# Two columns of W1I in one pass, scores read from PSUM, and the last bank stored whole

## The chip, the cores and the metric

The kernel runs on one core of a Trainium2 chip. The metric is the device time of one execution in microseconds (us); lower is better. The engines are named as the profile names them: PE (matmul) with PEld (its weight loads), DVE (vector), ACT (scalar), POOL, and SP, whose queue issues most DMAs. Each engine runs its own instructions strictly in the order in which the program holds them and waits for others by semaphores.

## The reference

```python
def reference(q, k, v, tau, moe..., moe2...):
    # q, k, v: 1 x 6016 x 256; w_in: 256 x 2048, w_out: 2048 x 256 (twice)
    qn = q / (norm(q, axis=1) + 1e-06);  kn = k / (norm(k, axis=1) + 1e-06)
    s = kn.transpose(0, 2, 1) @ qn / tau          # 256 x 256
    a = exp(s - s.max(-1));  a /= a.sum(-1) + 1e-09
    x = v @ a                                      # 6016 x 256
    h = x @ w1_in;  x = (h * sigmoid(1.702 * h)) @ w1_out
    h = x @ w2_in;  return (max(h, 0) + alpha * min(h, 0)) @ w2_out
```

All in float32. The kernel never makes `v @ a`: it multiplies `a` into the first layer's weight (`W1I = a @ w1_in`, called `WI` in the code) and feeds v's tokens to that.

## The kernel before

**Precision.** Every float32 operand is held as a pair hi + lo of fp32r tiles, and a product is three matmuls (`PASSES`): hi by hi, hi by lo, lo by hi. So each operand costs a cast on ACT (hi) and a subtraction on DVE (lo) before PE may use it.

**Head.** From 7 to 48 us PE accumulates the gram matrix k^T q in two PSUM banks, `gram[0]` and `gram[1]` (lines 340 to 349). At its end `nrm` holds the sums of squares, `rr` the reciprocal norms, and two matmuls spread q's reciprocal norms over the partitions into the PSUM bank `bc` (L447). ACT copies `bc` times 1/tau to `rq` (L448). `scores(m)` on DVE multiplies gram m by `rq` and k's factor and takes the maximum (L458); `exponent(m)` is on ACT (L463); `turn(m)` transposes the result on PE (`pt`, L472) and splits it into `eT_hi` (ACT, L477) and `eT_lo` (DVE, L476).

**W1I.** Output j of W1I (a column block of 256 of the 2048) is made by `make_w(j, m, ...)` for the two halves m: six matmuls of 256 columns each, `eT` by the converted weight `wi_pair[j]`, into a bank `pw` (L484). `keep_hi` (ACT, L492) and `keep_lo` (DVE, L496) store it to `WI`. The input weights come as raw 64-bit words, and a `Convert` piece turns them to hi and lo in steps: on ACT `scale` (L130) and `copy` (the cast to hi, L143), on DVE `shift` (L133), `signed` (L137), `power` (L147), `rest` (L150), `less` (L166) and `low` (L169, which writes lo). `ia[j]` is the piece of output j's input weight (outputs 4 and 5, and 6 and 7, share one of twice the width), `ob_[j]` that of the output weight. The `Converter` takes the pieces in one fixed order, ia1, ob0, ia2, ob1, ia3, ob2, ia4, ..., and does a step or two wherever the program calls `beside`; `conv.need(pieces)` emits at that place all steps still missing, up to those pieces.

**First token block.** `direct(j, outs, mid_way)` runs j from 0 to 7 over tokens 0 to 1023. Each has four units i = 0 to 3 (two rows of 128 features by two token chunks); here unit (j, i) names one. A unit is two `product` calls of three matmuls into a bank `ps_h` (L670) and, between them, two groups of three matmuls into `ps_o` for the unit (j-1, i) before (L699): 12 matmuls of 512 columns on PE. Then ACT applies the activation (`g`, L748) and casts `ghi` (L762), `mid_way(i)` is called, `beside` puts in some converter steps, and DVE makes `glo` (L768). `mid_way(1)` calls `emit_w(j + 1)`: the W1I of the next j is made behind unit (j, 1), two units ahead of its first use by unit (j + 1, 0).

**The rest.** All other tokens go through `quartet`, seven products for eight blocks (Strassen's way), for layer 1 and then layer 2. At the end `evacuate` copies the finished banks out; the last bank goes in two halves of 224 columns, each with its copy on ACT (L717) and its DMA on SP's queue (L718).

Of the kernel before, what the change touches and what calls it, by code (L numbers as in the profile page):

```python
# [8 lines left out]
F32 = mybir.dt.float32  # L9
F32R = mybir.dt.float32r  # L10
U32 = mybir.dt.uint32
AF = mybir.ActivationFunctionType
ALU = mybir.AluOpType
AX = mybir.AxisListType

P = 128
N = 6016
C = 256
FF = 2048
NT = FF // P  # L20
NQ = NT // 2
R = N // P
T = 512
# [11 lines left out]
TAIL = 12  # L35
ON_VECTOR = (4, 5, 6, 8)
assert sum(QK_PARTS) == R
PASSES = ((0, 0), (0, 1), (1, 0))
# [5 lines left out]
def f32(ap):  # L44
    return ap.bitcast(F32)
# [6 lines left out]
def flat(ap):  # L52
    return ap.rearrange("p a b -> p (a b)")
# [3 lines left out]
def attention_then_two_ffns(ctx: ExitStack, tc: tile.TileContext, q, k, vT, tau, w1i, w1o, w2i, w2o, alpha, outT):  # L57
# [14 lines left out]
    nc = tc.nc  # L72
# [12 lines left out]
    tau_sb = const.tile([P, 1], F32, name="tau_sb")  # L85
# [17 lines left out]
    class Convert:  # L103
# [64 lines left out]
        def low(self):  # L168
            nc.vector.tensor_tensor(self.lo, self.like(self.top), self.like(self.p), ALU.add)  # L169
            self.made = True  # L170
            if self.done:
                self.done()
# [73 lines left out]
    conv = Converter()  # L246
# [8 lines left out]
    with tc.manual_schedule():  # L255
# [2 lines left out]
        smx = ExitStack()  # L258
        Convert.pool = smx.enter_context(tc.tile_pool(name="cw", bufs=1, side="right"))
        sm = smx.enter_context(tc.tile_pool(name="sm", bufs=1, side="right"))  # L260
        wi_pair = {}

        def wi_tiles():
            return [sm.tile([P, 2, PIECE], F32R, tag=f"wi{h}", name=f"wi_{h}") for h in ("hi", "lo")]

        wi_first = [wi_tiles()]
        ident = sm.tile([P, P], F32, name="ident")
        ones = sm.tile([P, P], F32, name="ones")
        ET = tuple(sm.tile([P, 2, 2, P], F32R, name=f"eT_{h}") for h in ("hi", "lo"))

        def inner(j, n=1):
            def pair():
                if j % 2 == 0:
                    t = wi_first.pop() if wi_first else wi_tiles()
                    for i in range(2):
                        wi_pair[j + i] = tuple(x[:, :, i * C:(i + 1) * C] for x in t)
                    if n == 2:
                        return [flat(x) for x in t]
                return wi_pair[j]
            return Convert(w1i.rearrange("p (a n) -> p a n", a=2)[:, :, j * C:(j + n) * C], pair)  # L280
# [6 lines left out]
        ia, ob_ = {}, {}  # L287
# [8 lines left out]
        G = sm.tile([P, 2, C], F32, name="G")  # L296
# [3 lines left out]
        rs = sm.tile([P, 2], F32, name="rs")  # L300
# [12 lines left out]
        def operand(pool=None):  # L313
            if pool:
                return pool.tile([P, 2, T], F32R, tag="x", name="x")
            i = slot[0] % 11
            slot[0] += 1
            return xin[i > 3].tile([P, 2, T], F32R, tag=f"x{i}", name="x")
# [4 lines left out]
        def high(h, c):  # L323
            blocks[h, c] = operand()
            nc.scalar.copy(blocks[h, c][:, 0], raws[0, c][:, h])
# [5 lines left out]
        with ExitStack() as pre:  # L331
# [8 lines left out]
            gram = [pso.tile([P, T], F32, tag="o", name=f"gram{m}") for m in range(2)]  # L340
# [3 lines left out]
            def emit_gram(these, halves):  # L344
                for t in these:
                    i, r = rows[t]
                    for m in halves:
                        nc.tensor.matmul(gram[m][:, :C], tiles[i][:, 1, r, m * P:(m + 1) * P], tiles[i][:, 0, r, :],  # L348
                                         start=(t == 0), stop=(t == R - 1))
# [71 lines left out]
            rr = sm.tile([P, 4], F32, name="rr")  # L421
            high(0, 0)
            for h in range(2):
                add(norms[:, h], summed[:, h], acc[:, h])
                for j in range(2):
                    nc.tensor.matmul(nrm[:, 2 * h + j:2 * h + j + 1], norms[:, h, j * P:(j + 1) * P], ones[:, 0:1],  # L426
                                     start=True, stop=True)
            conv.steps(2)
            put_off.pop(0)()
            conv.steps(2)  # L430
            conv.load()
# [10 lines left out]
            bc = pso.tile([P, T], F32, tag="o", name="bc")  # L442
            rq = sm.tile([P, C], F32, name="rq")
            conv.steps(1)
            emit_gram(range(R - TAIL, R - TAIL + 4), (1,))
            for j in range(2):
                nc.tensor.matmul(bc[:, j * P:(j + 1) * P], rr[:, j:j + 1].to_broadcast([P, P]), ident, start=True, stop=True)  # L447
            nc.scalar.activation(rq, bc[:, :C], AF.Copy, scale=tau_sb)  # L448
            low(0, 0)
            high(1, 0)  # L450
        psh = ctx.enter_context(tc.tile_pool(name="psh", bufs=4, space=bass.MemoryType.PSUM))
        xin.append(ctx.enter_context(tc.tile_pool(name="xin1", bufs=1)))
        wti = ctx.enter_context(tc.tile_pool(name="wti", bufs=1))
# [1 line left out]
        WI = wti.tile([P, NQ, 2, 7, P], F32R, name="wi")  # L455

        def scores(m):
            nc.vector.tensor_tensor_reduce(G[:, m], gram[m][:, :C], rq, rr[:, 2 + m:3 + m], -3e38, ALU.mult, ALU.max,  # L458
                                           mx[:, m:m + 1])

        def exponent(m):
            nc.scalar.activation(mx[:, m:m + 1], mx[:, m:m + 1], AF.Copy, scale=-1.0)
            nc.scalar.activation(G[:, m], G[:, m], AF.Exp, bias=mx[:, m:m + 1], accum_out=sums[:, m:m + 1])  # L463
# [5 lines left out]
        def turn(m):  # L469
            pt = pso.tile([P, T], F32, tag="o", name="pt")  # L470
            for j in range(2):
                nc.tensor.transpose(pt[:, j * P:(j + 1) * P], G[:, m, j * P:(j + 1) * P], ident)  # L472
            hi, lo = (t[:, m].rearrange("p j c -> p (j c)") for t in ET)

            def rest():
                nc.vector.tensor_tensor(lo, pt[:, :C], f32(hi), ALU.subtract)  # L476
            nc.scalar.copy(hi, pt[:, :C])  # L477
            return rest

        def make_w(j, m, pw, at=0):  # L480
            n = 0
            for a, b in PASSES:
                for i in range(2):
                    nc.tensor.matmul(pw[:, at:at + C], ET[a][:, m, i], wi_pair[j][b][:, i],  # L484
                                     start=(n == 0), stop=(n == 5), skip_group_check=True)
                    n += 1
# [4 lines left out]
        def keep_hi(j, m, pw, at=0):  # L491
            nc.scalar.activation(next(kept(j, m)), pw[:, at:at + C], AF.Copy, scale=rs[:, m:m + 1])  # L492

        def keep_lo(j, m, pw, at=0):
            hi, lo = kept(j, m)
            nc.vector.scalar_tensor_tensor(lo, pw[:, at:at + C], rs[:, m:m + 1], f32(hi), ALU.mult, ALU.subtract)  # L496

        scores(0)
        exponent(0)
        emit_gram(range(R - TAIL + 4, R - 1), (1,))  # L500
        conv.steps(1)
        high(0, 1)
        scalar_work()
# [1 line left out]
        low(1, 0)  # L505
        low(0, 1)
        rest0 = turn(0)
        emit_gram((R - 1,), (1,))
        high(1, 1)
        rest0()  # L510
        assert ia[0].made and ia[1].made
# [105 lines left out]
        def combine_wi(j):  # L617
            return combine(*(WI[:, j, h, :4] for h in range(2)), *(lambda h=h: WI[:, j, h, S1:] for h in range(2)))

        def emit_w(j):  # L620

            conv.need([ia[j]])
            pw = psh.tile([P, T], F32, tag="h", name="pw") if j > 1 else pw_next
            for m in range(2):
                if j > 1 or m:
                    make_w(j, m, pw, m * C)
            for m in range(2):
                if j > 1 or m:
                    keep_hi(j, m, pw, m * C)
                    keep_lo(j, m, pw, m * C)  # L630
# [45 lines left out]
        acc_ps = {}  # L676
# [29 lines left out]
        def evacuate():  # L706

            while ready:
                l, c = ready.pop(0)
                n, t0 = WIDTHS[c], starts[c]  # L710
                for d in range(2):
                    dst = outT[d * P:(d + 1) * P, t0:t0 + n] if l else x1[c][:, d]
                    copies = (nc.scalar.copy, nc.vector.tensor_copy)
                    if l and d and c == len(WIDTHS) - 1:
                        for at in (slice(0, n // 2), slice(n // 2, n)):
                            ob = sp.tile([P, T], F32, tag="s", name="s", bufs=3)
                            nc.scalar.copy(ob[:, :n // 2], acc_ps[c][d][:, at])  # L717
                            nc.sync.dma_start(dst[:, at], ob[:, :n // 2])  # L718
                        continue
                    ob = sp.tile([P, T], F32, tag="ob", name="ob", bufs=4)  # L720
                    copies[d](ob[:, :n], acc_ps[c][d][:, :n])
                    nc.sync.dma_start(dst, ob[:, :n])
# [195 lines left out]
        for j in range(NQ):  # L918
            if j:
                conv.need([ob_[j - 1]])  # L920

            def mid_way(i):
                if j < NQ - 1 and i == 1:
                    if j == 0:
                        conv.need([ob_[0]])
                    emit_w(j + 1)
                if j == 2 and i == 0:
                    nc.sync.dma_start(alpha_sb, alpha)
                if j == 3 and i < 2:
                    load_tokens(0, 2 + i)  # L930
                if j == 5 and i == 0:
                    early, late = prepare(0, 1)
                    bg.extend(early + late)
                    for n in range(AHEAD):
                        combined.append(combine_wi(n))
                        bg.extend(combined[n])

            outs = direct(j, outs, mid_way)
# [4 lines left out]
        sp = ctx.enter_context(tc.tile_pool(name="sp", bufs=3, side="right"))  # L943
# [143 lines left out]
```

## Time and profile before

| | before |
|---|---|
| time, median of 3 runs (lowest to highest) | 1034.88 us (1034.62 to 1034.90) |
| the profiled execution: its own time / its span | 1034.92 us / 1033.2 us |
| PE busy | 1027.2 us (99%) |
| DVE busy / ACT busy | 766.1 us (74%) / 753.5 us (73%) |
| chain that ended last, by engine | PE 99% |
| matmuls on PE | 4664 |

Times in the rows count from the first instruction of the span. Matmuls are pipelined: a row's duration is longer than the distance to the next matmul, so what one costs is read from the distance between starts, or from the chain, whose pieces do not overlap.

### The profile page before, as it was taken

Reading aid. Unit: us, or ns where it says so; the run is one execution under the profiler, and the core shown is the slowest. Engines: PE = TensorE matmul, PEld = TensorE weight load, DVE = VectorE, ACT = ScalarE, POOL = GpSimd, SP = SyncE. Lnnn points to the kernel's source line nnn. Section 1 sums busy time; section 2 is a strip of 40 time slices with the busy share of each in tenths; the row PEclk is TensorE's granted clock in tenths of the full one; section 3 lists DMA queues with packets and bytes.
Section 4 is the critical chain, followed back from the end, with each engine's and each line's share of the span. In section 5 each row is a group of like instructions: output and inputs, shape, how many; then the busy total and the mean of one; then the engine's idle time right before and its main releaser. Section 6 shows DMA issues by size and latency. Waiting matters only on the chain.

```text
span 1033.2 us, 12543 instructions
## 1 busy us (share of the span) xinstructions
PE 1027.2 (99%) x4664; PEld 868.0 (84%) x4664; DVE 766.1 (74%) x1233; ACT 753.5 (73%) x1259; POOL 31.3 (3%) x42
## 2 busy tenths in 40 slices
PE   9999999999999999999999999999999999999998
PEld 8888888888888888888998888888888888888997
DVE  5789977878778787445637777787877787877765
ACT  6776667778777777666767777777777777867776
POOL 4400000000000000000110000000000000000000
PEclk9999999999999999999999999999999999999999
DMA  9635012125224323003543001001001000000101
GB/s 359 242 105 180 1 63 96 41 77 179 77 82 158 99 95 133 0 1 122 204 169 113 1 21 62 1 21 62 0 21 62 1 18 25 35 1 1 42 0 36
DMA packets 30605, 77.62 MB, mean 75 GB/s; under 512 B 3024, under 2 KB 7760, under 8 KB 30288
## 3 DMA queue, kind: packets, MB, share of 16 engines
q1 hardware_dynamic: 28240, 65.29, 18.1%
q0 software_dynamic: 2304, 11.54, 3.3%
q8 instruction: 36, 0.59, 0.2%
q14 instruction: 25, 0.20, 0.1%
HBM read 52.96 MB, written 23.86 MB: 74 GB/s over the span
## 4 chain that ended last, share of the span: by engine, by line
PE 99%; DMA 0%; SPq 0%; issue 0%; ACT 0%; ACTq 0%
PE ps_o L699 50%; PE ps_h L670 44%; PE gram L348 4%; PE pw L484 1%; DMA qk<-in_k 0%; SPq L368 0%; PE nrm L426 0%; PE bc L447 0%; PE pt L472 0%; ACT s L717 0%; ACTq L1083 0%
## 5 line engine op out<-in xcount | busy, mean ns | idle before, releaser
L699 PE MATMUL ps_o<-ghi,wo 128*128 128x512 f32 (+1 forms) x1536 | 562.5, 386 | 0.0
L670 PE MATMUL ps_h<-x,wi 128*128 128x512 f32 (+1 forms) x2040 | 550.7, 386 | 0.0
L670 PEld LDWEIGHTS ps_h<-x,wi 128*128 128x128 f32 x2040 | 382.2, 188 | 71.8 <-DVE wi L496 0.4
L699 PEld LDWEIGHTS ps_o<-ghi,wo 128*128 128x128 f32 x1536 | 288.6, 188 | 53.6
L699 PE MATMUL ps_o<-glo,wo 128*128 128x512 f32 (+1 forms) x768 | 296.5, 386 | 0.0
L737 DVE TENSOR_TENSOR g<-ps_h,s 128x512 f32<-128x512 f32 (+1 forms) x177 | 120.1, 678 | 94.0 <-PE ps_h L670 60.4
L766 DVE SCALAR_TENSOR_TENSOR glo<-g,sign_sb,ghi 128x512 fp32r<-128x512 f32 (+1 forms) x192 | 141.4, 737 | 55.4 <-ACT ghi L760 51.1
L803 ACT COPY s<-ps_h 128x512 f32<-128x512 f32 (+1 forms) x177 | 102.2, 577 | 104.6 <-PE ps_h L670 100.4
L768 DVE TENSOR_TENSOR glo<-g,ghi 128x512 fp32r<-128x512 f32 (+1 forms) x192 | 126.4, 677 | 67.5 <-ACT ghi L762 67.1
L699 PEld LDWEIGHTS ps_o<-glo,wo 128*128 128x128 f32 x768 | 144.3, 188 | 26.9 <-DVE glo L766 0.3
L760 ACT ACTIVATE ghi<-g,sign_sb 128x512 fp32r<-128x512 f32 (+1 forms) x192 | 137.0, 714 | 16.3 <-DVE g L756 10.9
L762 ACT CAST ghi<-g 128x512 fp32r<-128x512 f32 (+1 forms) x192 | 113.2, 611 | 3.6
L748 ACT ACTIVATE g<-ps_h 128x512 f32<-128x512 f32 (+1 forms) x112 | 65.5, 585 | 37.4 <-PE ps_h L670 36.7
L752 ACT ACTIVATE g<-g,sign_sb 128x512 f32<-128x512 f32 (+1 forms) x97 | 69.5, 717 | 29.1 <-DVE g L737 28.6
L756 DVE SCALAR_TENSOR_TENSOR g<-g,slope_sb 128x512 f32<-128x512 f32 (+1 forms) x97 | 71.6, 739 | 16.8 <-ACT g L752 16.6
L756 DVE SCALAR_TENSOR_TENSOR g<-ps_h,slope_sb,g 128x512 f32<-128x512 f32 (+1 forms) x95 | 69.7, 734 | 0.0
L814 ACT COPY ps_h<-ps_h 128x512 f32<-128x512 f32 (+1 forms) x87 | 49.0, 563 | 28.4 <-PE ps_h L670 27.8
L752 ACT ACTIVATE g<-ps_h,sign_sb 128x512 f32<-128x512 f32 (+1 forms) x95 | 64.2, 676 | 2.0 <-PE ps_h L670 0.2
L748 ACT ACTIVATE g<-g 128x512 f32<-128x512 f32 (+1 forms) x80 | 49.8, 623 | 15.5 <-DVE g L737 15.3
L348 PE MATMUL gram<-qk 128*128 128x256 f32 x156 | 34.3, 381 | 1.0 <-DMA qk<-in_k 1.0
L348 PEld LDWEIGHTS gram<-qk 128*128 128x128 f32 x156 | 29.5, 190 | 5.2 <-issue 1.4
L561 DVE TENSOR_TENSOR x<-t,x 128x512 fp32r<-128x512 f32 (+1 forms) x44 | 29.0, 672 | 0.0
(104 smaller groups left out, 504.7 us busy)
## 6 DMA issues: line engine op xcount, KB each, us to landing
wi<-w2i POOLq DMA_DIRECT2D x8, 896.0 KB, 4.9
xraw<-in_vT SPq DMA_DIRECT2D x10, 512.0 KB, 6.1
x<-ob SPq DMA_DIRECT2D x20, 256.0 KB, 2.4
xraw<-x SPq DMA_DIRECT2D x10, 512.0 KB, 3.5
out_T<-ob SPq DMA_DIRECT2D x20, 256.0 KB, 2.1
qk<-in_q SPq DMA_DIRECT2D x9, 512.0 KB, 10.2
qk<-in_k SPq DMA_DIRECT2D x9, 512.0 KB, 10.3
raw<-in_w2i SPq DMA_DIRECT2D x8, 512.0 KB, 4.1
```

What stands on the lines that cost most here:

```text
L348: nc.tensor.matmul(gram[m][:, :C], tiles[i][:, 1, r, m * P:(m + 1) * P], tiles[i][:, 0, r, :], start=(t == 0), stop=(t == R - 1))
L670: nc.tensor.matmul(ps[:, :n], WI[:, wq, a, blk], x[:, b, :n], start=(start and i == 0), stop=(stop and i == 2), skip_group_check=True)
L699: nc.tensor.matmul(acc_ps[c][d][:, :n], WO[:, j, a, f, d * P:(d + 1) * P], (hi, lo)[b][:, :n], start=(start and i == 0), stop=(stop and i ...
L737: nc.vector.tensor_tensor(self.src, ps[:, :self.n], s[:, :self.n], ALU.add)
L748: nc.scalar.activation(self.g, self.src, AF.Gelu_apprx_sigmoid)
L752: nc.scalar.activation(self.g, self.src, AF.Copy, scale=sign_sb[:, self.f])
L756: nc.vector.scalar_tensor_tensor(self.g, self.src, slope_sb[:, self.f], self.g, ALU.mult, ALU.max)
L760: nc.scalar.activation(self.hi, self.g, AF.Copy, scale=sign_sb[:, self.f])
L762: nc.scalar.copy(self.hi, self.g)
L766: nc.vector.scalar_tensor_tensor(self.lo, self.g, sign_sb[:, self.f], f32(self.hi), ALU.mult, ALU.subtract)
L768: nc.vector.tensor_tensor(self.lo, self.g, f32(self.hi), ALU.subtract)
L803: nc.scalar.copy(s[:, :n], ps[:, :n])
```

## The change

Three edits. First, `emit_pair(j)` makes outputs j and j + 1 of W1I at once, with matmuls of 512 columns and one bank for each half m, and with one `hi` and one `lo` instruction for each half. Outputs 2 to 7 go this way: `mid_way(2)` of j = 1, 3 and 5 calls `emit_pair(j + 1)`; output 1 stays with `emit_w`. Second, in the head ACT copies `gram[0]` to `G` early, 1/tau goes into k's factors `rr[:, 2:4]`, `scores(0)` reads q's factors from `bc` itself, and the copy to `rq` comes behind `exponent(0)`; one step of the gram moves behind the first transposes. Third, the last bank is stored by one copy and one DMA.

```diff
@@ inner / head
-                    t = wi_first.pop() if wi_first else wi_tiles()
+                    t = wi_whole[j] = wi_first.pop() if wi_first else wi_tiles()
...
             conv.steps(2)
+            nc.scalar.copy(G[:, 0], gram[0][:, :C])
             put_off.pop(0)()
...
-            nc.scalar.activation(rq, bc[:, :C], AF.Copy, scale=tau_sb)
-            low(0, 0)
-            high(1, 0)
+            nc.vector.tensor_scalar(rr[:, 2:4], rr[:, 2:4], tau_sb, None, ALU.mult)
...
         def scores(m):
-            nc.vector.tensor_tensor_reduce(G[:, m], gram[m][:, :C], rq, rr[:, 2 + m:3 + m], ...
+            nc.vector.tensor_tensor_reduce(G[:, m], *((gram[1][:, :C], rq) if m else (G[:, 0], bc[:, :C])), rr[:, 2 + m:3 + m], ...
...
         scores(0)
         exponent(0)
-        emit_gram(range(R - TAIL + 4, R - 1), (1,))
+        nc.scalar.copy(rq, bc[:, :C])
+        high(1, 0)
+        low(0, 0)
+        emit_gram(range(R - TAIL + 4, R - 2), (1,))
...
         rest0 = turn(0)
-        emit_gram((R - 1,), (1,))
+        emit_gram((R - 2, R - 1), (1,))
@@ W1I
+        def emit_pair(j):
+            conv.need([ia[j], ia[j + 1]])
+            for m in range(2):
+                pw = psh.tile([P, T], F32, tag="h", name="pw")
+                for n, (a, b, i) in enumerate((a, b, i) for a, b in PASSES for i in range(2)):
+                    nc.tensor.matmul(pw, ET[a][:, m, i], wi_whole[j][b][:, i], start=(n == 0), stop=(n == 5))
+                hi, lo = (WI[:, j:j + 2, h, 2 * m:2 * m + 2] for h in range(2))
+                src = pw.rearrange("p (j a b) -> p j a b", j=2, a=2)
+                nc.scalar.activation(hi, src, AF.Copy, scale=rs[:, m:m + 1])
+                nc.vector.scalar_tensor_tensor(lo, src, rs[:, m:m + 1], f32(hi), ALU.mult, ALU.subtract)
...
             def mid_way(i):
-                if j < NQ - 1 and i == 1:
-                    if j == 0:
-                        conv.need([ob_[0]])
-                    emit_w(j + 1)
+                if j == 0 and i == 1:
+                    conv.need([ob_[0]])
+                    emit_w(1)
+                if j < NQ - 1 and j % 2 and i == 2:
+                    emit_pair(j + 1)
@@ evacuate
-                        for at in (slice(0, n // 2), slice(n // 2, n)):
-                            ob = sp.tile([P, T], F32, tag="s", name="s", bufs=3)
-                            nc.scalar.copy(ob[:, :n // 2], acc_ps[c][d][:, at])
-                            nc.sync.dma_start(dst[:, at], ob[:, :n // 2])
+                        ob = sp.tile([P, T], F32, tag="s", name="s", bufs=3)
+                        nc.scalar.copy(ob[:, :n], acc_ps[c][d][:, :n])
+                        nc.sync.dma_start(dst, ob[:, :n])
```

DVE before, from the `glo` of unit (1, 0) to that of unit (1, 2), in `direct(1)`. The two L496 rows are the `keep_lo` of output 2; `low` of ia3 is L169.

```order
L768 TENSOR_TENSOR glo<-g,ghi 128x512
L166 TENSOR_TENSOR top<-top,wo 128x512
...
L137 SCALAR_TENSOR_TENSOR top<-raw,p 128x512
L147 TENSOR_SCALAR p<-top 128x512
L768 TENSOR_TENSOR glo<-g,ghi 128x512
L496 SCALAR_TENSOR_TENSOR wi<-pw,rs,wi 128x256 x2
L150 SCALAR_TENSOR_TENSOR p<-raw,p 128x512
L166 TENSOR_TENSOR top<-top,wi_hi 128x512
L169 TENSOR_TENSOR wi_lo<-top,p 128x2x256
L768 TENSOR_TENSOR glo<-g,ghi 128x512
```

DVE in the change at the same place (L781 is now `glo`, L632 the store of lo for the pair 2 and 3).

```order
L137 SCALAR_TENSOR_TENSOR top<-raw,p 128x512
L147 TENSOR_SCALAR p<-top 128x512
L781 TENSOR_TENSOR glo<-g,ghi 128x512
L150 SCALAR_TENSOR_TENSOR p<-raw,p 128x512
L166 TENSOR_TENSOR top<-top,wi_hi 128x512
L169 TENSOR_TENSOR wi_lo<-top,p 128x2x256
L781 TENSOR_TENSOR glo<-g,ghi 128x512
L632 SCALAR_TENSOR_TENSOR wi<-pw,rs,wi 128x2x256 x2
```

The two `keep_lo` of output 2 are gone from behind the second `glo`; the last three steps of ia3 stand there, and all else keeps its order up to L169.

PE in the change, behind unit (1, 1): unit (1, 2), then the first half of the pair (L684 is now `ps_h`, L713 `ps_o`, L628 `pw`). Before, the matmuls of output 2 stood ahead of these twelve.

```order
L684 MATMUL ps_h<-x,wi 128x512 x3
L713 MATMUL ps_o<-ghi,wo 128x512
L713 MATMUL ps_o<-glo,wo 128x512
L713 MATMUL ps_o<-ghi,wo 128x512
L684 MATMUL ps_h<-x,wi 128x512 x3
L713 MATMUL ps_o<-ghi,wo 128x512
L713 MATMUL ps_o<-glo,wo 128x512
L713 MATMUL ps_o<-ghi,wo 128x512
L628 MATMUL pw<-wi_hi,eT_hi 128x512 x2
L628 MATMUL pw<-wi_lo,eT_hi 128x512 x2
L628 MATMUL pw<-wi_hi,eT_lo 128x512 x2
```

W1I of output 2 moved one unit later, and the third matmul there now reads the lo of ia3 (as well as of ia2).

## Rows read from the trace of the kernel before

**Rows 1.** The page, its head and part 1: busy us (share of the span), instructions.

```profile
span 1033.2 us, 12543 instructions
PE 1027.2 (99%) x4664; PEld 868.0 (84%) x4664; DVE 766.1 (74%) x1233; ACT 753.5 (73%) x1259; POOL 31.3 (3%) x42
```

**Rows 2.** The chain in order of time (start us, us, what).

```profile
47.80 0.22 PE pt L472 x2
...
63.29 1.44 PE pw L484 x12
...
66.11 0.68 PE ps_h L670 x3
```

**Rows 3.** The timeline of PE (start us, us, engine, line, operation), behind unit (1,1).

```profile
63.12 0.40 PE L484 MATMUL pw<-wi_hi,eT_hi 128*128 128x256 f32 x2
```

**Rows 4.** The timeline of DVE in `direct(1)`, from unit (0,3)'s conversions on.

```profile
58.57 0.68 DVE L137 SCALAR_TENSOR_TENSOR top<-raw,p 128x512 uint32<-128x512 uint32 x1
...
67.35 0.69 DVE L137 SCALAR_TENSOR_TENSOR top<-raw,p 128x512 uint32<-128x512 uint32 x1
...
68.42 0.68 DVE L768 TENSOR_TENSOR glo<-g,ghi 128x512 fp32r<-128x512 f32 x1
69.02 0.48 DVE L496 SCALAR_TENSOR_TENSOR wi<-pw,rs,wi 128x256 fp32r<-128x256 f32 x1
...
70.44 0.69 DVE L150 SCALAR_TENSOR_TENSOR p<-raw,p 128x512 f32<-128x512 uint32 x1
71.04 0.69 DVE L166 TENSOR_TENSOR top<-top,wi_hi 128x512 f32<-128x512 f32 x1
71.76 0.69 DVE L169 TENSOR_TENSOR wi_lo<-top,p 128x512 fp32r<-128x512 f32 x1
```

**Rows 5.** The timeline of ACT in the same stretch.

```profile
66.40 0.62 ACT L762 CAST ghi<-g 128x512 fp32r<-128x512 f32 x1
...
69.90 0.61 ACT L143 CAST wi_hi<-top 128x512 fp32r<-128x512 f32 x1
```

**Rows 6.** Stretches: us; busy PE, PEld, DVE, ACT, POOL; granted clock; DMA.

```profile
58.57:65.80 7.23, 7.23 (x39) 6.20 (x38) 6.99 (x14) 5.23 (x11) 0.00 (x0) 1.00 0.24 73
1030.00:1031.00 1.00, 0.00 (x0) 0.00 (x0) 0.00 (x0) 0.00 (x0) 0.00 (x0) 1.00 0.99 356
1031.50:1032.00 0.50, 0.00 (x0) 0.00 (x0) 0.00 (x0) 0.00 (x0) 0.00 (x0) 0.52 0.23 72
```

**Rows 7.** The timeline of PE at the start of the span.

```profile
1.07 3.93 PE L308 MATMUL idle<-ones 128*128 128x128 f32 x20 [1.07 <-POOL ones L301]
4.84 1.03 PE L348 MATMUL gram<-qs 128*128 128x256 f32 x4
6.89 1.32 PE L348 MATMUL gram<-qk 128*128 128x256 f32 x5 [1.02 <-DMA qk<-in_k]
```

**Rows 8.** The timeline of all engines at the end of the head.

```profile
44.81 0.47 ACT L448 ACTIVATE rq<-bc,tau_sb 128x256 f32<-128x256 f32 x1 [0.54 <-PE bc L447]
...
45.31 0.48 DVE L458 CUSTOM_DVE_ANT_0 G<-gram,rq,rr 128x256 f32<-128x256 f32 x1
...
46.08 0.51 ACT L463 ACTIVATE G<-G,mx 128x256 f32<-128x256 f32 x1
...
47.09 0.68 ACT L130 ACTIVATE p<-raw 128x512 f32<-128x512 f32 x1
...
48.05 0.37 ACT L477 CAST eT_hi<-pt 128x256 fp32r<-128x256 f32 x1 [0.28 <-PE pt L472]
...
48.47 0.51 PE L484 MATMUL pw<-wi_hi,eT_hi 128*128 128x256 f32 x2
```

**Rows 9.** The timeline of the span's end (SPq is SP's DMA queue).

```profile
1028.72 0.53 ACT L721 COPY ob<-ps_o 128x448 f32<-128x448 f32 x1 [0.71 <-PE ps_o L699]
...
1029.34 0.59 ACT L717 COPY s<-ps_o 128x224 f32<-128x224 f32 x2
1029.71 0.90 SPq L718 DMA_DIRECT2D out_T<-s  x2
```

More of the change, by code (lines that the diff above doesn't have):

```diff
@@ L260, in attention_then_two_ffns @@
         sm = smx.enter_context(tc.tile_pool(name="sm", bufs=1, side="right"))
-        wi_pair = {}
+        wi_pair, wi_whole = {}, {}
         def wi_tiles():
@@ L457, in scores @@
         def scores(m):
-            nc.vector.tensor_tensor_reduce(G[:, m], gram[m][:, :C], rq, rr[:, 2 + m:3 + m], -3e38, ALU.mult, ALU.max,
+            nc.vector.tensor_tensor_reduce(G[:, m], *((gram[1][:, :C], rq) if m else (G[:, 0], bc[:, :C])), rr[:, 2 + m:3 + m], -3e38, ALU.mult, ALU.max,
                                            mx[:, m:m + 1])
```

## The prediction

> **What bounds the kernel now.** The page first: PE is busy 99% of a span of 1033.2 us, DVE and ACT three quarters [rows 1]. Busy says little for pipelined matmuls, so the chain comes next: its pieces lie end to end, and its shares are PE 99%. A matmul of 512 columns costs 0.68/3 = 0.227 us there and one of 256 columns 1.44/12 = 0.120 us [rows 2]. From 7 us on PE is never without work except a few tenths at the end of the head, so the time is what PE has queued plus what PE is made to wait. A change can win by taking columns or matmuls off PE, and it loses every microsecond for which PE stands, because nothing later has slack to give it back. The last view is therefore the timelines of the engines that feed PE where the change moves work: DVE and ACT in the first token block. There DVE is busy 6.99 of 7.23 us [rows 6], and it is late: its `glo` of unit (1,1) begins at 68.42 [rows 4], while PE had ended unit (1,1) at 63.12 [rows 3]. PE doesn't feel that lag of 5.3 us, since it reads that `glo` one whole `direct` later. It would feel it if it asked DVE for something new at once.
>
> **Part 1, the columns.** Six outputs by 12 matmuls of 256 columns become 36 of 512. Two of the old cost 2 x 0.120 = 0.240, one of the new 0.227 [rows 2]: 36 x 0.0133 = 0.48 us less on PE, all of it on the path. The stores on ACT and DVE are halved in number, which lies beside PE and is worth nothing by itself. The Trainium skill ("TensorE: Matmul & The Clock Gate", § Wait — 56ns, not 53.3ns?) puts the fixed cost of a warm matmul at about 2.5 ns over its columns; by that the 36 saved matmuls would give an estimated 0.09 us. The rows show 13 ns for each, five times that, so the measurement decides; by the page the sum below would be 0.4 us dearer.
>
> **Part 2, the pair's inputs.** `emit_pair(2)` needs both ia2 and ia3, and it stands behind unit (1,2). PE gets there after unit (1,1), at 63.12 [rows 3], and one unit of 12 matmuls, 12 x 0.227 = 2.72: at 65.84. It wants three things.
>
> The hi of ia3 for its first matmul. ACT makes it (L143) from what L137 on DVE writes; that L137 runs from 67.35 to 68.04 [rows 4], ACT is through with its `ghi` at 67.02 [rows 5], so the cast can run from 68.06 to 68.68 (0.61 long at 69.90 [rows 5]).
>
> The lo of ia3 for its third matmul, which PE would reach at 65.84 + 0.45 = 66.29. In the program's order DVE comes to it behind the `glo` of unit (1,1), as before, but without the two `keep_lo` between. So L150 starts where L496 did, at 69.02, L166 0.60 later at 69.62 (the distance 70.44 to 71.04), L169 0.72 later at 70.34 (71.04 to 71.76), and it ends 0.69 later, at 71.03 [rows 4]. DVE cannot be sooner: the 17 instructions from 58.57 up to the `glo` at 68.42 stand in the same order in the change, in the trace they follow each other with hardly a gap [rows 6], and none of them waits for anything that moves earlier. Add 0.05 for the semaphore and 0.11 that a matmul takes longer when it begins after a wait (0.51 for the two at 48.47 against 0.40 [rows 8, 3]): PE resumes at an effective 71.19 instead of 66.29. **PE stands 4.9 us.** Two matmuls run in between, at 68.7, when hi is there.
>
> Who waits behind it: everything on PE, and through it ACT's store of hi and DVE's of lo. Their cover is unit (1,3), 2.72 us: the first half of the pair ends near 72.2 and its hi and lo (0.7 each) are there by 73.8; the second half ends near 73.6 and is stored by 75.1; unit (2,0) starts at 76.1. So no second wait follows. At outputs 4 and 6 both inputs come as one piece of double width, whose L169 stands 13 DVE instructions ahead of the pair's store in the program's order, and DVE, which worked on while PE stood, is by then some 3 us less behind. I cost them at nothing; if that cover is gone, PE waits for the pair's store at the next unit.
>
> **Part 3, the clock.** PE is without matmuls about 2.6 us, then runs two, then stands 1.9 us more. In this trace the granted clock was still 1.00 from 1030 to 1031 and half (0.52) from 1031.5 on [rows 6], some 2.2 us after the last matmul (the last copy begins at 1029.34 [rows 9]); a pause of 1.02 us at 5.87 to 6.89 left no trace in the rate of what follows (5 matmuls of the gram in 1.32) [rows 7]. So a fall from 2.4 to 1.2 GHz within the wait is likelier than not. Its price, by the only row with PE at the lower level: the 20 matmuls of 128 columns at the start took 4.84 - 1.07 = 3.77 us [rows 7] where 0.11 each [rows 2] makes 2.2, so 1.6 us went until the clock was up. Ends: 0.6 us if it rises soon after PE resumes, 2.4 if half as late again; I take 1.5, near the row.
>
> **Part 4, the head.** `scores(0)` no longer waits for the copy to `rq` (44.81 and 0.47 long, DVE at 45.31 [rows 8]); it can start when `bc` is there, some 0.46 sooner, and the exponent at 45.62. But on ACT the copy to `rq` and one more cast now stand between the exponent and the cast to `eT_hi`. Exponent and cast took 1.01 together (46.08 to 47.09), so: 45.62 + 1.01 + 0.51 for the second cast + 0.4 to 0.47 for the copy + 0.68 = 48.25, where `eT_hi` began at 48.05 [rows 8]. PE waits for it as now, and comes no earlier: +0.2 us. Ends: -0.2 (the 0.19 that PE stands ahead of 48.47 goes) and +0.5 (each instruction on ACT takes its whole row). The early copy of `gram[0]` lies ahead of the square root on ACT and costs a tenth at most, within these ends.
>
> **Part 5, the end.** Copy whole: 0.53 instead of two in 0.59 [rows 9]. The second of two issues (0.90 for both) goes, so the last DMA is issued near 1029.92 instead of 1030.20; it carries twice the bytes. -0.1 us, between 0 and -0.3.
>
> **Sum.** -0.48 + 4.9 + 1.5 + 0.2 - 0.1 = +6.0 us. The profiled execution took 1034.92 for its span of 1033.2, and the median of the runs is 1034.88, so the two can stand for one another: 1034.9 + 6.0 = **1040.9 us**.
>
> **Rivals.** (a) The wait without the fall of the clock: PE has two matmuls in the middle, and the one pause of the trace that ended in a fall was followed by no work at all. Then 1034.9 + 4.5 = 1039.4 us. (b) PE finds its inputs ready, and the change only saves columns: 1034.9 - 0.48 + 0.1 = 1034.5, not slower. It decides at 66.29: that is so if L169 of ia3 ends by then, 4.7 us sooner than rows 4 make it. For it: before, the converter was in time for output 2, whose 12 matmuls ran without a wait in 1.44 [rows 2]. Against it: that was output 2 alone, DVE's rows leave no gap to take up 4.7 us, and its order in the change puts only the two `keep_lo` out of the way. (c) The pairs at 4 and 6 wait as well, for banks and stores: the pair takes two of four `ps_h` banks and leaves one unit of cover where there were two. Up to 1.5 us each, 1043.9. Against it: DVE stands closer behind PE after the first wait.
>
> **How the numbers follow.** The forecast has 0.56 (1040.0 to 1041.8 by its ends), (a) 0.30 (1039.0 to 1039.9), (b) 0.06, (c) 0.08. The range 1038.8 to 1041.9 holds the first two but for a few in a hundred, and leaves out (b) and (c). Faster or slower begins at 0.2%, 2.07 us, about what a measurement of this kernel can tell from no change: all but (b) is slower, 0.93; (b) is the same, 0.06; 0.01 for faster.
>
> **What would show it.** In the trace of the change PE waits behind unit (1,2) first for ACT's cast of ia3 and then for DVE's L169, 4 to 5 us in all, and L169 ends 7.9 us after the point where unit (1,1) ended on PE. The pairs at 4 and 6 take 12 matmuls in 2.72 us without a wait. The granted clock in the 5 us behind the wait tells the forecast from (a). If PE runs through the first pair without a wait, my reading of DVE's order is wrong and the time is near 1034.5.

## The result, and the profile after

| | before | after |
|---|---|---|
| time, median of 6 runs each (lowest to highest) | 1034.89 us (1034.62 to 1035.01) | 1041.15 us (1040.75 to 1042.07) |
| ratio to before, 95% interval | | 1.0062 [1.0049, 1.0075] |
| profiled execution: time / span | 1034.92 / 1033.2 us | 1040.75 / 1039.0 us |
| matmuls on PE | 4664 | 4628 |

The change makes the kernel 6.3 us slower. One execution in all that follows, 3707.7 us of the kernel with the first pair one unit earlier, stands apart for a reason not known and is left out of its median. The head of the page of after, beside [rows 1]:

```profile
span 1039.0 us, 12461 instructions
PE 1030.0 (99%) x4628; PEld 867.4 (83%) x4628; DVE 765.2 (74%) x1228; ACT 753.0 (72%) x1253; POOL 31.3 (3%) x42
```

PE has 36 matmuls fewer and still reads 99%: an average over a millisecond hides 5 us. The list of PE's waits over the whole span shows them at once. (Engine, tile, line, what it waited for: us in total, times, longest; a third, of 1.1 us, stands at the start of the span in both kernels.)

```profile
PE pw L628 <- ACT wi_hi L143: 2.5, 1, 2.5
PE pw L628 <- DVE wi_lo L169: 1.6, 1, 1.6
```

Both at the new line L628, once each: the first of the three pairs. The timeline of PE and DVE there, to be laid beside [rows 3, 4]:

```profile
65.80 0.39 PE L713 MATMUL ps_o<-ghi,wo 128*128 128x512 f32 x1
...
67.26 0.69 DVE L137 SCALAR_TENSOR_TENSOR top<-raw,p 128x512 uint32<-128x512 uint32 x1
67.98 0.62 ACT L143 CAST wi_hi<-top 128x512 fp32r<-128x512 f32 x1 [1.05 <-DVE top L137]
...
68.33 0.69 DVE L781 TENSOR_TENSOR glo<-g,ghi 128x512 fp32r<-128x512 f32 x1
...
68.66 0.73 PE L628 MATMUL pw<-wi_hi,eT_hi 128*128 128x512 f32 x2 [2.47 <-ACT wi_hi L143]
68.93 0.68 DVE L150 SCALAR_TENSOR_TENSOR p<-raw,p 128x512 f32<-128x512 uint32 x1
...
69.53 0.68 DVE L166 TENSOR_TENSOR top<-top,wi_hi 128x512 f32<-128x512 f32 x1
...
70.25 0.69 DVE L169 TENSOR_TENSOR wi_lo<-top,p 128x512 fp32r<-128x512 f32 x1
...
71.00 1.22 PE L628 MATMUL pw<-wi_lo,eT_hi 128*128 128x512 f32 x2 [1.61 <-DVE wi_lo L169]
...
72.02 1.05 PE L628 MATMUL pw<-wi_hi,eT_lo 128*128 128x512 f32 x2
...
72.87 1.05 PE L628 MATMUL pw<-wi_hi,eT_hi 128*128 128x512 f32 x2
```

PE is through with unit (1,2) at 65.80 + 0.23. It gets the hi of ia3 at 68.66 and its lo at 71.00. DVE goes from one conversion step to the next without rest, as before. The last two rows show something else: two matmuls of 512 columns now take 0.85 us from start to start (72.02 to 72.87), 0.43 each and not 0.227. The stretches of after, read as [rows 6]:

```profile
66.00:68.60 2.60, 0.19 (x1) 0.00 (x0) 2.53 (x6) 1.51 (x4) 0.00 (x0) 1.00 0.69 202
68.60:71.00 2.40, 0.74 (x3) 0.30 (x3) 2.37 (x5) 1.12 (x3) 0.00 (x0) 1.00 0.00 0
71.00:71.50 0.50, 0.50 (x1) 0.50 (x2) 0.50 (x1) 0.00 (x0) 0.00 (x0) 0.52 1.32 123
71.50:73.00 1.50, 1.50 (x5) 1.12 (x4) 0.04 (x1) 0.00 (x0) 0.00 (x0) 0.50 0.86 317
73.00:74.40 1.40, 1.40 (x5) 1.11 (x4) 0.57 (x1) 0.69 (x1) 0.00 (x0) 0.50 0.89 363
74.40:75.00 0.60, 0.60 (x4) 0.48 (x4) 0.18 (x1) 0.00 (x0) 0.00 (x0) 0.97 0.02 7
```

The granted clock is 1.00 through the wait itself and drops to half (1.2 GHz) just as PE resumes; it is up again at 74.4. While PE stood, a half clock would have cost nothing.

The later pairs wait for nothing. One of them in the chain of after:

```profile
96.27 0.69 PE ps_o L713 x3
96.95 2.73 PE pw L628 x12
99.68 0.68 PE ps_h L684 x3
```

Twelve matmuls in 2.73 us, where two outputs took 2 x 1.44 [rows 2].

### The profile page after: what moved, and what is told of

Same layout as the page of the kernel before. It is cut to its first block, busy times and chain, and to the rows that moved or that the text cites. A ratio compares the mean times of both kernels' runs of the same rounds, so it can differ in the third digit from the quotient of the medians.

```text
span 1039.0 us, 12461 instructions
## 1 busy us (share of the span) xinstructions
PE 1030.0 (99%) x4628; PEld 867.4 (83%) x4628; DVE 765.2 (74%) x1228; ACT 753.0 (72%) x1253; POOL 31.3 (3%) x42
## 4 chain that ended last, share of the span: by engine, by line
PE 98%; DVE 1%; ACT 0%; issue 0%; POOL 0%; DVEq 0%; POOLq 0%
PE ps_o L713 49%; PE ps_h L684 43%; PE gram L348 4%; PE pw L628 1%; PE idle L308 0%; PE pw L483 0%; DVE top L137 0%; DVE glo L781 0%; DVE p L150 0%; DVE top L166 0%; ACT L921 0%; DVE p L147 0%; ACT g L761 0%; ACT wi L491 0%; DVE wi_lo L169 0%
## 5 line engine op out<-in xcount | busy, mean ns | idle before, releaser
L713 PE MATMUL ps_o<-ghi,wo 128*128 128x512 f32 (+1 forms) x1536 | 561.6, 385 | 0.0
L684 PE MATMUL ps_h<-x,wi 128*128 128x512 f32 (+1 forms) x2040 | 550.6, 385 | 0.0
L684 PEld LDWEIGHTS ps_h<-x,wi 128*128 128x128 f32 x2040 | 382.4, 188 | 72.6 <-DVE wi L495 0.4
L713 PEld LDWEIGHTS ps_o<-ghi,wo 128*128 128x128 f32 x1536 | 288.4, 188 | 53.4
L713 PE MATMUL ps_o<-glo,wo 128*128 128x512 f32 (+1 forms) x768 | 296.2, 386 | 0.0
L781 DVE TENSOR_TENSOR glo<-g,ghi 128x512 fp32r<-128x512 f32 (+1 forms) x192 | 126.4, 677 | 68.2 <-ACT ghi L775 67.9
L713 PEld LDWEIGHTS ps_o<-glo,wo 128*128 128x128 f32 x768 | 144.2, 188 | 27.6 <-DVE glo L781 0.4
```

The lines of the kernel that those rows point to most:

```text
L684: nc.tensor.matmul(ps[:, :n], WI[:, wq, a, blk], x[:, b, :n], start=(start and i == 0), stop=(stop and i == 2), skip_group_check=True)
L713: nc.tensor.matmul(acc_ps[c][d][:, :n], WO[:, j, a, f, d * P:(d + 1) * P], (hi, lo)[b][:, :n], start=(start and i == 0), stop=(stop and i ...
L781: nc.vector.tensor_tensor(self.lo, self.g, f32(self.hi), ALU.subtract)
```

## The experiments

Theory W: PE stands because DVE comes to ia3's lo only at 70.25, and the rest costs the clock. Rival B: the pair as such is dear, with two of four banks, wide stores and one unit of cover. Rival H: the new order in the head sets DVE's lag. All eight kernels below ran beside the kernel before, at 1035.0 us; the change itself was not run again with them, so a comparison with its 1041.15 is one of medians. Each edit is shown against the change, the head alone and the end alone against the kernel before.

**The pairs alone** (head and end as before).

```diff
-            nc.scalar.copy(G[:, 0], gram[0][:, :C])
...
-            nc.vector.tensor_scalar(rr[:, 2:4], rr[:, 2:4], tau_sb, None, ALU.mult)
+            nc.scalar.activation(rq, bc[:, :C], AF.Copy, scale=tau_sb)
...
```

> The kernel before with the pairs alone, head and end as before. Theory W (PE stands behind unit (1,2) because DVE comes to ia3's low only then, and the clock falls in the wait): 1041.0 us, the whole loss of the change, PE standing 4 to 5 us at L628 or its line here. Rival H (the new order in the head costs more than its 0.2 us and sets the lag of DVE): about 1036 to 1038.

Measured: 1041.63 us, ratio 1.0065 [1.0049, 1.0082]. In its trace PE waits 2.5 us for ACT's cast of ia3 and 1.6 us for DVE's L169 at L626, the pair's line there, as in after. The pairs carry the whole loss; H falls.

**ia3 ahead of ob1 in the converter's order.**

```diff
-        conv.todo = [ia[1], ob_[0], ia[2], ob_[1], ia[3], ob_[2], ia[4], ...]
+        conv.todo = [ia[1], ob_[0], ia[2], ia[3], ob_[1], ob_[2], ia[4], ...]
```

> The change with one edit: the converter takes ia3 ahead of ob1. Theory W: DVE's L169 of ia3 moves from 70.25 to about 66.2 and ends at 66.9, PE gets there at 66.5, so the wait shrinks from 4.9 to about 0.5 us and the clock stays up: 1035.2 us. Rival B (the pair itself is dear: two banks of four, wide stores, one unit of cover): stays near 1041. A wait for ob1 in its place is not expected (ready near 71, wanted near 72.7).

Measured: 1035.05 us, ratio 1.0002 [0.9992, 1.0011]. The timelines of PE and DVE in this kernel:

```profile
65.96 0.63 PE L628 MATMUL pw<-wi_hi,eT_hi 128*128 128x512 f32 x2
...
66.87 0.74 PE L628 MATMUL pw<-wi_lo,eT_hi 128*128 128x512 f32 x2 [0.28 <-DVE wi_lo L169]
67.45 0.63 PE L628 MATMUL pw<-wi_hi,eT_lo 128*128 128x512 f32 x2
```

and DVE's step that ends its wait:

```profile
66.13 0.68 DVE L169 TENSOR_TENSOR wi_lo<-top,p 128x512 fp32r<-128x512 f32 x1
```

L169 ends at 66.81 instead of 70.94, PE waits for it a few tenths, and the matmuls behind it keep their 0.23. All three pairs, both banks and the wide stores are still there, so B falls: what costs is the date at which DVE is through with ia3. ob1, moved back, made no new wait.

**Matmuls into the wait**, on a tile of ones, to keep PE at work.

```diff
+            def fill(n):
+                for _ in range(n):
+                    nc.tensor.matmul(banks[1][:, :P], ones, ones, start=True, stop=True)
...
+                if j == 2 and m == 0:
+                    fill(12)
...
+                    if j == 2 and m == 0 and n == 2:
+                        fill(8)
...
```

> The change with 20 matmuls of 128 columns on a tile of ones put into the wait: 12 ahead of the first pair's first matmul, 8 ahead of its third, into the bank that the second half clears. They stand where PE waits anyway. Theory W with the clock: the granted clock stays at 1.00 and the time falls by the 1.7 us that the trace shows at half rate, to 1039.4. Rival (the slow matmuls behind the wait have another cause than PE's rest): no gain, 1041.2, or up to 0.4 more for the matmuls themselves.

Measured: 1039.12 us (1038.88 to 1039.95), ratio 1.0041 [1.0026, 1.0056]; 2.0 us under the change. Each of the 20 shows as two matmuls in the trace. Two stretches of this kernel, read as [rows 6]:

```profile
66.00:68.60 2.60, 2.60 (x26) 2.60 (x24) 2.53 (x6) 1.51 (x4) 0.00 (x0) 1.00 0.62 195
...
71.50:73.00 1.50, 1.50 (x8) 1.24 (x7) 0.18 (x1) 0.69 (x1) 0.00 (x0) 1.00 0.92 374
```

and its timeline of PE, where the line is L638:

```profile
65.89 2.84 PE L629 MATMUL pw<-ones 128*128 128x128 f32 x24
...
70.86 0.73 PE L638 MATMUL pw<-wi_lo,eT_hi 128*128 128x512 f32 x2
71.43 0.63 PE L638 MATMUL pw<-wi_hi,eT_lo 128*128 128x512 f32 x2
```

The clock stays at 1.00 and the third matmul still starts at 70.86 (71.00 in after, whose first token block begins 0.16 later): DVE's date is the same, the wait is filled, and only the slow stretch behind it is gone. So the loss has two parts, some 5 us of standing and 1.5 to 2 us of clock, less the half microsecond that the pairs save.

**The first pair one unit earlier.**

```diff
-                if j < NQ - 1 and j % 2 and i == 2:
+                if j < NQ - 1 and j % 2 and i == (1 if j == 1 else 2):
```

> The change with the first pair one unit earlier, behind unit (1,1) instead of (1,2). DVE's order up to ia3's L169 is the same, PE arrives 2.7 us sooner. Theory W: the wait grows by 2.4 to 2.7 us (7.3 to 7.6 in all), time 1043.7 with the same price of the clock. Rival B: the pair gets its two units of cover back, so 1036 to 1039.

Measured: 1043.9 us (median of three executions), ratio 1.0086 [1.0069, 1.0102]. The timeline of PE:

```profile
62.98 0.39 PE L713 MATMUL ps_o<-ghi,wo 128*128 128x512 f32 x1
68.88 1.22 PE L628 MATMUL pw<-wi_hi,eT_hi 128*128 128x512 f32 x2 [5.50 <-ACT wi_hi L143]
71.22 1.22 PE L628 MATMUL pw<-wi_lo,eT_hi 128*128 128x512 f32 x2 [1.12 <-DVE wi_lo L169]
```

PE comes 2.8 us sooner (62.98 against 65.80) and resumes at the same time (71.22 against 71.00); the loss grows by 2.8 us. More cover for the stores, which B wanted, bought nothing.

**The head alone.**

```diff
+            nc.scalar.copy(G[:, 0], gram[0][:, :C])
...
-            nc.scalar.activation(rq, bc[:, :C], AF.Copy, scale=tau_sb)
-            low(0, 0)
-            high(1, 0)
+            nc.vector.tensor_scalar(rr[:, 2:4], rr[:, 2:4], tau_sb, None, ALU.mult)
...
```

> The kernel before with the head's edit alone. By the prediction's part 4: +0.2 us, 1035.1 (ends 1034.7 to 1035.4), since ACT reaches the cast to eT_hi no sooner. Rival (the shorter way to the scores reaches PE): 1034.5 or less.

Measured: 1034.82 us, ratio 1.0002 [0.9994, 1.0011]. The times can't tell +0.2 from -0.2. PE's timeline in this kernel:

```profile
47.23 0.38 PE L471 MATMUL pt<-ident,G 128*128 128x128 f32 x2
47.45 1.03 PE L348 MATMUL gram<-qs 128*128 128x256 f32 x4
48.40 0.51 PE L483 MATMUL pw<-wi_hi,eT_hi 128*128 128x256 f32 x2
```

`pw` starts at 48.40, before at 48.47 [rows 8]. From the first `nrm` matmul to `pw` it is 6.97 us before, 6.83 here and in three of the other kernels with the new head, but 7.1 to 7.2 in `ia3_sooner` and after, where PE reached `nrm` earliest (41.23 in after, 41.58 here). Those two lose it on DVE, in front of the new order: the first reciprocal of `rr`, which starts the way to the scores, stands behind a conversion step, L150. Here DVE is free and waits for ACT's square root `rt` (first row); in after it is still at the conversion (the other two rows):

```profile
42.87 0.18 DVE L436 RECIPROCAL rr<-rt 128x4 f32<-128x4 f32 x1 [0.27 <-ACT rt L433]
...
42.26 0.69 DVE L150 SCALAR_TENSOR_TENSOR p<-raw,p 128x512 f32<-128x512 uint32 x1
42.87 0.17 DVE L436 RECIPROCAL rr<-rt 128x4 f32<-128x4 f32 x1
```

The reciprocal starts 1.29 us after `nrm` here and 1.64 in after. From it to `pw` it is 5.53 to 5.55 us in all six kernels with the new head and 5.58 to 5.65 in the four with the old: the new head gains 0.03 to 0.12.

**The end alone.**

```diff
-                        for at in (slice(0, n // 2), slice(n // 2, n)):
...
+                        nc.scalar.copy(ob[:, :n], acc_ps[c][d][:, :n])
+                        nc.sync.dma_start(dst, ob[:, :n])
```

> The kernel before with the last bank stored whole, nothing else. Part 5: -0.1 us, 1034.8 (1034.6 to 1034.9). Rival (a DMA of twice the bytes lands later than the two): +0.1 to +0.4.

Measured: 1034.97 us, ratio 1.0000 [0.9992, 1.0009]. The end of its timeline:

```profile
1028.97 0.37 PE L699 MATMUL ps_o<-ghi,wo 128*128 128x448 f32 x1
...
1029.37 0.53 ACT L716 COPY s<-ps_o 128x448 f32<-128x448 f32 x1
1029.93 0.33 SPq L717 DMA_DIRECT2D out_T<-s  x1
```

From the last matmul's start to the end of the span it is 4.13 us here (1028.97 to 1033.1) and 4.21 before: a gain of 0.1, below what the times can show. In all, it is 4.13 to 4.18 in the seven kernels with the new end and 4.21 to 4.23 in the three with the old.

**The first pair undone** (outputs 2 and 3 one by one, the rest of the change kept), and **late pairs** (the same with the old head, whose lines are left out here).

```diff
-                if j == 0 and i == 1:
-                    conv.need([ob_[0]])
-                    emit_w(1)
-                if j < NQ - 1 and j % 2 and i == 2:
+                if j < 3 and i == 1:
+                    if j == 0:
+                        conv.need([ob_[0]])
+                    emit_w(j + 1)
+                if j in (3, 5) and i == 2:
                     emit_pair(j + 1)
```

> The change with outputs 2 and 3 made one by one again, as before; pairs stay for 4 and 5 and for 6 and 7. Theory W: no wait is left, the pairs save 2 x 0.16 us: 1034.9 - 0.32 + 0.2 - 0.1 = 1034.7. Rival B (pairs cost as such): 1036 to 1039.

> The same with the head as before: pairs for 4 to 7 and the last bank whole. By the sum 1034.9 - 0.32 - 0.1 = 1034.5, a little under the kernel before; by the page's 2.5 ns for a matmul, an estimate from the Trainium skill, 1034.7.

Measured: 1034.55 us, ratio 0.9996 [0.9987, 1.0005], and 1034.37 us (1033.90 to 1034.64), ratio 0.9994 [0.9985, 1.0003]. Taking back one of three pairs takes back the whole loss. The second kernel has the lowest median of all, 0.6 us under the kernel before, but its interval contains 1, so it is not shown to be faster. In the traces the two kept pairs are a gain: from the first `ps_o` matmul to the last matmul it is 970.61 us before (58.33 to 1028.94) and 970.13 in late pairs (58.10 to 1028.23), 0.48 less. The other two traces without pairs have 970.61 and 970.63, the first pair undone has 970.11.

## Why the prediction was right

It gave 1040.9 us, in a range of 1038.8 to 1041.9; measured 1041.15, with one of the six executions above the range. In the profiled executions the pieces add up to 5.8 us: the first `ps_o` matmul starts 0.08 sooner (58.25 for 58.33), from there to the last matmul it is 5.94 longer (976.55 for 970.61), and the end is 0.04 shorter. Parts 1 and 4 came out a few tenths shorter than forecast and the clock, by the medians, a few tenths dearer. That these cancel is luck; the large term, the wait, is not.

**Part 2, the wait,** came out as worked. L169 of ia3 was to end 7.9 us after the end of unit (1,1) on PE; in after it is 63.03 to 70.94, 7.9. The time that PE loses there, from the starts in the trace of after: 2.6 us before the hi, 1.8 before the lo, 0.2 for the two matmuls that begin after a wait, and 0.25 that the prediction did not count, a wait for a `glo` at 64.07 which PE now reaches sooner. The sum is 4.9. The last piece came not on top of the forecast, because the date on which PE resumes is set by DVE: what PE waits earlier it does not wait later. That the wait is the distance between DVE's date and PE's is shown three ways: DVE's step moved up 4.1 us takes the wait away but for a few tenths, PE moved up 2.8 us adds 2.8, filling the wait leaves PE's restart where it was.

One reading of the prediction was wrong, in a name and not in the sum: the `glo` at 68.42 is that of unit (1,0), not (1,1). The two `keep_lo` that `mid_way(1)` emits stand behind it and ahead of the `glo` of (1,1), so the excerpt of DVE before runs from the `glo` of unit (0,3) to that of (1,1). Two rows of before, the first where PE is through with unit (1,0), and two of after:

```profile
60.37 0.84 PE L670 MATMUL ps_h<-x,wi 128*128 128x512 f32 x3
72.37 0.69 DVE L768 TENSOR_TENSOR glo<-g,ghi 128x512 fp32r<-128x512 f32 x1
...
63.34 0.68 DVE L781 TENSOR_TENSOR glo<-g,ghi 128x512 fp32r<-128x512 f32 x1
64.07 0.50 PE L713 MATMUL ps_o<-glo,wo 128*128 128x512 f32 x1
```

So DVE's lag was 8.0 us (60.37 to 68.42) at unit (1,0) and not 5.3, and the `direct` by which PE reads later covered it only just: when unit (1,2) came 1.5 us sooner, it had to wait for the `glo` of (0,2). The date of L169 was worked out from the order of the instructions, which was read rightly.

**Part 3, the clock,** was right in kind and size: eight matmuls at or near 0.427 instead of 0.227 make 1.6 us in the profiled execution, 1.5 was forecast. The fall came as PE resumed and not within the wait. Where it did come within it, in the kernel with the pair one unit earlier, the matmuls behind the wait are slow until about 74 as well, so the price does not turn on that here. With the wait filled, the medians differ by 2.0. The profiled execution is the fastest of the six, and the other five have a mean granted clock of 0.996 where it has 0.998; that they pay a little more for the clock fits this, but no trace of them shows it.

**Part 1** held: a pair takes 2.73 us for 2 x 1.44. Over the whole trace two pairs give 0.48, where the sum had 0.32; the extra 0.16 is not explained by the rows read here. The 2.5 ns that the Trainium skill gives as the fixed cost of a warm matmul ("TensorE: Matmul & The Clock Gate", § Wait — 56ns, not 53.3ns?) would have made it an estimated 0.06 for two pairs; the traces, with 0.48, speak against it for this kernel.

**Part 4** is the one term with the wrong sign: the new head is 0.03 to 0.12 shorter from the reciprocal to `pw`, not 0.2 longer, which its ends allowed. In after, `pw` starts 0.07 sooner. The step that failed is the length of ACT's chain, here in after:

```profile
46.12 0.35 ACT L499 COPY rq<-bc 128x256 f32<-128x256 f32 x1
46.37 1.14 ACT L325 CAST x<-xraw 128x512 fp32r<-128x512 f32 x2
47.41 0.68 ACT L130 ACTIVATE p<-raw 128x512 f32<-128x512 f32 x1
47.99 0.35 ACT L476 CAST eT_hi<-pt 128x256 fp32r<-128x256 f32 x1
```

The copy to `rq` took 0.25 from start to start (46.12 to 46.37) where 0.4 to 0.47 had been set down, and L130 took 0.58 (47.41 to 47.99) where its whole row, 0.68, had been. So `eT_hi` began at 47.99, not 48.25. **Part 5** was -0.03 to -0.1, where -0.1 was forecast.

Of the rivals, (a) is what the filled wait gives, 1039.1 for a forecast of 1039.4: the mechanism was priced right, it only did not happen by itself. (b) would have needed L169 by 66.29; moving ia3 up brought it to 66.81, and the time to 1035.05, near that rival's 1034.5. (c), waits at the pairs for 4 and 6, did not happen.

## What to carry to other kernels

Where an engine runs late without harm because its results are read much later, that lag is a debt: an edit that asks it for something new at once pays it as a wait, here 4.9 us. So before merging two steps into one, ask when the later of the inputs is made in its engine's own order, not whether the engine has room on average. And a wait of a few microseconds on PE costs more than itself here, since the matmuls behind it ran at half clock; filling it with idle matmuls brought the clock's part back, 2.0 us, and moving one conversion up brought back nearly all.

## What the runs showed of the hardware

In after the granted clock did not fall while PE stood, but as it resumed: it is 1.00 in the stretch from 68.6 to 71.0, with 0.74 us of work in 2.4, then 0.50 under full work until 74.4. With a longer rest (the pair one unit earlier) it fell inside it: the stretch from 63.5 to 68.5, without a matmul, has a mean of 0.88, and 0.50 follows until about 74.

```profile
63.50:68.50 5.00, 0.00 (x0) 0.00 (x0) 4.90 (x10) 3.70 (x7) 0.00 (x0) 0.88 0.45 137
68.50:71.10 2.60, 1.22 (x2) 0.50 (x2) 2.57 (x5) 1.01 (x2) 0.00 (x0) 0.50 0.00 0
71.20:74.00 2.80, 2.78 (x7) 2.20 (x8) 0.00 (x0) 0.67 (x1) 0.00 (x0) 0.50 0.96 309
74.20:75.00 0.80, 0.80 (x5) 0.62 (x5) 0.60 (x1) 0.00 (x0) 0.00 (x0) 1.00 0.28 113
```
